# The left output projection of a segmented memory attention: from products of 256 columns to products of 512

## The chip, the cores and the metric

The kernel runs on one core of one Trainium2 chip. The metric is the device time of one execution in microseconds; the figure of a kernel is the median of its timed runs.

Five engines work from queues of their own: PE (matrix products, with the weight loads listed apart as PEld), DVE (the vector engine), ACT (the scalar engine), POOL (GpSimd) and SP, which here only issues transfers. PE adds its products up in PSUM; DVE and ACT read PSUM, POOL and the transfers do not, so what POOL works on has to lie in SBUF, the on-chip working memory.

## The reference, cut to what matters

A layer-normed sequence `xn` of 2048 rows and 1024 columns goes through two branches that are added to `x`. Branch A is attention over 64 segments of 32 rows, with 8 memory rows in front of each; the attention output of the memory rows is the memory of the next segment, so the segments depend on each other in a chain.

```python
for s in range(n_seg):                                  # 64 segments
    h = concat([mem, xs], axis=1)                       # 8 memory rows + 32 rows
    q, k, v = h @ Wq, h @ Wk, h @ Wv                    # 32 heads of 128
    p = softmax(where(mask, q @ k.T * scale, -1e9))
    o = einsum('bhte,hed->btd', p @ v, Wo)              # output projection
    mem = o[:, :M, :].copy()
    outs.append(o[:, M:, :])
...
return x + A(xn, mem0, ...) + B(xn, ...)
```

Branch B takes the two rows of `xn` with the highest routing score through a gated feed-forward of 3584 and adds the result to these two rows.

## The kernel before, in words

**Tiling.** A segment's step takes 32 rows, the 8 memory rows and the first 24 of its own 32 rows; the last 8 rows of a segment (its "left" rows) do not fit into a tile of 32 and are set apart. The left rows of four consecutive segments make one more tile of 32 rows; such a set of four is called a group (G), and j = 0 to 3 is the segment's place in it. The weights are cut into 64 granules of 128 partitions x 2048 columns: granules 0 to 47 are Wq, Wk and Wv in six phases of eight (`PHASES`), granules 48 to 63 are Wo, two heads each. 44 granules stay in SBUF for the whole run; the 20 of `STREAMED` come in anew for every segment, through five slots (the tile `g`). SP issues them in a fixed order, each as soon as a slot is free.

**A segment's step.** For each phase p and granule kc, four products of 32 rows x 512 columns go to four groups of 32 PSUM rows (line 788, `PSm`); they run at the same time on four strips of PE's columns. Then ACT casts `PSm` to bf16 (`XB`, line 807), PE transposes it in the next phase, and the scores of a head half are formed at (2, 6) and (4, 6), their exponent taken on ACT (line 666) and softened on DVE (lines 671 to 694) at (3, 4) and (5, 0). The pair (p, kc) names a place in the program: what is hooked there is issued behind the products of granule 8p + kc. After phase 5 come the 16 granules of Wo (place (6, w)), written to `WO` by `project`, line 574: eight products of 256 columns per granule. Line 856 adds `WO` to the input rows; this is the last DVE work of the step, and the next segment's memory comes out of it.

**The left rows.** Their projections are made from granules that are in SBUF anyway, as extra passes between the products of the main rows. The table `PASSES` says at which place (j, p, kc) which granules are passed; a unit ("q0", "k0" and so on, and "o" for the output projection) has one PSUM bank, `psL`, and the units follow each other in it. `COPIES` says where a finished unit is taken out of the bank. Unit "o" begins in the fourth segment of a group, in (6, 3) to (6, 14) with five passes, goes on with three at (7, 0) and two at (8, 0), that is, around the end of the segment, and is finished in the next group's first segment (j = 0) with six more. In the last segment of all, the sixteen passes of "o" stand between those of `WO`, and the sum follows at the end.

**The left output projection, before.** `one_pass` calls the same `project` as the main rows, with `lhs_left` (line 578) as weights: for each of a granule's two heads, four products of 256 columns, one for each quarter of the 1024 output columns, to rows 32 g to 32 g + 31 of the tile `WL`. Rows 32 g hold columns 256 g to 256 g + 255. `copy_unit` at (0, 4, 3) adds the bank to `OL`, which holds the left rows of x in the same arrangement (`load_left`, `sum_left`), in one DVE operation (line 596), and POOL stores four blocks (line 599).

**What sets the order.** The schedule is written by hand: every engine runs its instructions in the order in which the code issues them. Tiles of one name tag share one buffer (`one` is a pool with one buffer for each tag), so a tile may be written only when the last reader of the tile before it in that tag is done. `OTL`, the attention output of the left rows, is in tag "otl"; `OL` and `STL`, the next group's left rows as weights, share the tag "stl".

Of the kernel before, what the change touches and what calls it, by code (L numbers as in the profile page):

```python
# [8 lines left out]
BF16 = mybir.dt.bfloat16  # L9
F32 = mybir.dt.float32  # L10
U32 = mybir.dt.uint32
ALU = mybir.AluOpType
# [31 lines left out]
}  # L44

COPIES = {"q0": (1, 1, 0, "scalar"), "q1": (1, 5, 7, "vector"), "k0": (2, 2, 0, "scalar"), "k1": (3, 1, 0, "scalar"),
          "v0": (3, 4, 7, "scalar"), "v1": (3, 5, 7, "scalar"), "o": (0, 4, 3, "vector")}


@with_exitstack  # L50
def kernel(
# [16 lines left out]
    nc = tc.nc  # L68
    P = 128
    Bsz, S, D = A_x.shape  # L70
    H, E = A_Wq.shape[1], A_Wq.shape[2]
    M = A_mem0.shape[1]
    SEG = int(A_seg_len)
# [9 lines left out]
    XM = SEG - M  # L83
# [34 lines left out]
    one = ctx.enter_context(tc.tile_pool(name="one", bufs=1, reuse_waits="tile"))  # L118
# [78 lines left out]
    for s in range(4):  # L197
        nc.vector.tensor_copy(out=SELM[:, s, :, 0:XM],
                              in_=IDENT[:, 32 * s:32 * s + XM].unsqueeze(1).to_broadcast([P, 4, XM]))
        nc.vector.tensor_copy(out=SELL[:, s, :, :],  # L200
                              in_=IDENT.rearrange("p (s c) -> p s c", c=32)[:, :, XM:SEG])
# [113 lines left out]
        PTm = turn(OB)  # L315
        nc.vector.tensor_copy(out=gview(st)[:, :, :, XM:SEG], in_=PTm[:, :, :, XM:SEG])

    def load_left(G, t):
        o4 = x2[4 * G * SEG:4 * (G + 1) * SEG, :].rearrange("(s r) d -> s r d", s=4)
        for g in range(4):  # L320
            nc.gpsimd.dma_start(out=t[32 * g:32 * (g + 1), :], in_=o4[:, XM:SEG, 256 * g:256 * (g + 1)])
        return t

    def norm_left(t, G):
# [230 lines left out]
    def one_pass(u, g, Gv):  # L555
        if u not in units:
            begin(u)
        PS, n = units[u]
        units[u][1] = n - 1
        if u == "o":  # L560
            project(PS, g - 48, Gv, lhs_left, n == 1, first=(n == 16))
        else:
            left_pass(PS, g, Gv, n == 8, n == 1)

# [5 lines left out]
    def project(PS, w, Gv, lhs, last, first=False):  # L570
        for hs in range(2):
            h = 2 * w + hs
            for g in range(4):
                nc.tensor.matmul(PS[32 * g:32 * g + 32, 0:256], lhsT=lhs(h),  # L574
                                 rhs=Gv[:, D * hs + 256 * g:D * hs + 256 * (g + 1)], start=(first and hs == 0),
                                 stop=(last and hs == 1), tile_position=(0, 32 * g), skip_group_check=True)

    def lhs_left(h):
        return otl_of[0][:, h, :, :].rearrange("p s r -> p (s r)")

    xl_of, otl_of = [None], [None]

    def copy_unit(u, s, engine):
        PS, n = units.pop(u)
        assert n == 0, (u, s, n)
        Gu = group_of(u, s)
        copy = nc.scalar.copy if engine == "scalar" else nc.vector.tensor_copy
        half = int(u[-1]) if u != "o" else 0
        if u[0] == "v":
            new_vl[half] = one.tile([P, 512], BF16, tag=roles[half], name="VL")  # L590
            copy(out=new_vl[half][:, :], in_=PS[:, :])
            if half:
                roles.insert(0, roles.pop())
        elif u == "o":
            OL = xl_of[0]
            nc.vector.tensor_tensor(out=OL[:, :], in0=PS[:, 0:256], in1=OL[:, :], op=ALU.add)
            o4 = out2[4 * Gu * SEG:4 * (Gu + 1) * SEG, :].rearrange("(s r) d -> s r d", s=4)
            for g in range(4):
                nc.gpsimd.dma_start(out=o4[:, XM:SEG, 256 * g:256 * (g + 1)], in_=OL[32 * g:32 * (g + 1), :])
        else:  # L600
            XBl = one.tile([P, 512], BF16, tag=roles[0], name="XBl")
            copy(out=XBl[:, :], in_=PS[:, :])
            stores.append(lambda: nc.scalar.dma_start(out=ql_d[Gu][2 * half + "qk".index(u[0])], in_=XBl[:, :]))
            if engine == "scalar":
                stores.pop()()

    for s in range(NSEG):
# [227 lines left out]
        for w in range(16):  # L835
            if w == 5:
                attend(1, 0)
            if w == 8 and s + 1 < NSEG:
                attend(1, 1, lambda: turned.append(turn_rows(xn, left_too)))
                nxt["st"], stl = new_st(turned[0])  # L840
                STL = stl or STL
            elif w == 8:
                attend(1, 1)
            Gv = granule(48 + w)
            project(WO, w, Gv, lhs_main, w == 15, first=(w == 0))
            held[48 + w] = Gv
            run_passes(6, w)
            if w == 9 and s + 1 < NSEG:
                new_lx(s + 1)
                bring_back(1, nc.scalar.copy)  # L850
                bring_back(2, nc.vector.tensor_copy)
            if w == 11 and j == 3:
                xl_of[0] = load_left(G, one.tile([P, 256], BF16, tag="stl", name="OL")[:, :])
            release(6, w)
        OB = X[s % 2]
        nc.vector.tensor_tensor(out=OB[:, :], in0=WO[:, 0:256], in1=OB[:, :], op=ALU.add)  # L856
# [127 lines left out]
```

## Time and profile before

| | |
|---|---|
| median of 3 timed runs | 1893.73 us (1885.0 to 1897.26) |
| profiled execution, its own time | 1889.55 us |
| its span from first to last instruction | 1887.9 us |
| PE busy / weight loads busy | 1574.1 us (83%) / 882.6 us (47%) |
| DVE / ACT / POOL busy | 880.0 / 681.9 / 441.4 us |
| moved by DMA | 712.41 MB, mean 377 GB/s |
| streamed granules | 1134 transfers of 512 KB, 63 of 256 KB |
| granted PE clock, mean | 0.955 |

The page is one profiled execution. Busy shares are averages over stretches with different limits, so stretches of single segments are read too: a table of windows gives, for each, its length, the busy time and the number of instructions of each engine, the granted clock, the share of time that the 16 DMA engines were busy, and the rate. In lists, "[1.17 <-DMA g<-wsc]" behind an instruction means that its engine stood idle for 1.17 us before it and that the transfer into `g` ended that; "issue" stands where the profile names nothing that the engine waited for. Tile names are the program's (`WL<-g,OTL` writes WL from g and OTL), shapes are partitions x elements.

### The profile page before, as it was taken

The page shows a single profiled execution, that of the slowest core. Times are in us where ns is not written, and L with a number is a line of the kernel's source. Part 1 is how long each engine was busy: PE and PEld are TensorE (multiplying, and loading weights), DVE is VectorE, ACT ScalarE, POOL GpSimd, SP SyncE. Part 2 cuts the span into 40 slices and gives each one's busy share as a digit, 9 for nine tenths or more (in the row PEclk, how much of TensorE's full clock was granted, in tenths as well). Part 3 has the DMA queues.
Part 4 walks back from the last instruction along what each step waited for, and adds up shares of the span by engine and source line. Part 5 has one row for each costly group of instructions (what it writes and reads, how often), then busy time and mean ns, then how long its engine had stood idle before and what let it go on. Part 6 is the DMA issues. An engine that isn't in the chain of part 4 may idle for free.

```text
span 1887.9 us, 82457 instructions
## 1 busy us (share of the span) xinstructions
PE 1574.1 (83%) x36000; PEld 882.6 (47%) x36000; DVE 880.0 (47%) x2913; ACT 681.9 (36%) x1916; POOL 441.4 (23%) x882
## 2 busy tenths in 40 slices
PE   3458889888888898888888988888998888989864
PEld 1134545454454444545454544545454454545433
DVE  6725444545354444544454344445544454455430
ACT  1123433344334343433333334333433443434320
POOL 3111223222131322213121321312132131312220
PEclk8669999999999999999999999999999999999995
DMA  9999999999999999999999999999999999999998
GB/s 369 400 363 381 366 384 383 395 388 371 364 374 394 354 387 384 378 389 363 394 374 381 367 359 371 362 391 368 381 375 367 381 383 382 372 392 380 389 406 327
DMA packets 232122, 712.41 MB, mean 377 GB/s; under 512 B 39296, under 2 KB 53168, under 8 KB 231760
## 3 DMA queue, kind: packets, MB, share of 16 engines
q1 hardware_dynamic: 194384, 671.18, 93.0%
q0 software_dynamic: 28736, 28.09, 4.7%
q10 hardware_dynamic: 8640, 7.87, 1.2%
q8 instruction: 282, 4.62, 0.9%
q14 instruction: 80, 0.66, 0.1%
HBM read 694.32 MB, written 22.29 MB: 380 GB/s over the span
## 4 chain that ended last, share of the span: by engine, by line
DMA 57%; PE 38%; DVE 2%; issue 2%; SPq 0%; ACT 0%; ACTq 0%; DVEq 0%
DMA g<-wsc 50%; PE PSm L788 21%; PE PSl L567 5%; PE WO L574 5%; PE BT L624 3%; PE WL L574 2%; DMA XP<-in_A_x_dram 2%; DMA MW<-in_B_w_gate_dram 1%; DMA MW<-in_B_w_up_dram 1%; DVE XR L248 1%; DMA g<-in_A_Wq_dram 1%; DMA wres<-in_A_Wo_dram 1%; DMA g<-in_B_w_down_dram 1%; DMA g<-in_A_Wo_dram 1%; PE BT L293 1%
## 5 line engine op out<-in xcount | busy, mean ns | idle before, releaser
L788 PE MATMUL PSm<-wres,ST 128*32 128x512 bf16 x8448 | 706.7, 384 | 10.6 <-issue 4.0
L788 PEld LDWEIGHTS <-ST 128*32 128x32 bf16 x12288 | 326.0, 96 | 402.7 <-issue 172.9
L788 PE MATMUL PSm<-g,ST 128*32 128x512 bf16 x3588 | 362.6, 387 | 101.0 <-DMA g<-wsc 75.5
L574 PEld LDWEIGHTS <-OT 128*32 128x32 bf16 x8192 | 221.2, 98 | 159.6 <-issue 140.2
L807 ACT CAST XB<-PSm 128x512 bf16<-128x512 f32 x256 | 150.1, 586 | 309.7 <-PE PSm L788 306.8
L574 PE MATMUL WO<-wres,OT 128*32 128x256 bf16 x5632 | 240.7, 281 | 17.5 <-issue 8.8
L483 POOL DMA_DIRECT2D LX<-ql_d x63 | 33.6, 533 | 813.7 <-PE WO L574 339.2
L574 PE MATMUL WO<-g,OT 128*32 128x256 bf16 x2560 | 134.4, 284 | 83.8 <-DMA g<-wsc 73.7
L567 PE MATMUL PSl<-wres,STL 128*32 128x512 bf16 x2112 | 184.2, 389 | 0.0
L858 POOL DMA_DIRECT2D out_dram<-X x256 | 129.5, 513 | 217.9 <-DVE X L856 174.6
L639 DVE COPY KT<-BT 128x512 bf16<-128x512 bf16 x112 | 45.9, 410 | 282.5 <-ACT XB L807 114.5
L273 POOL DMA_DIRECT2D X<-in_A_x_dram x256 | 129.6, 510 | 183.8 <-PE PSm L788 70.7
L377 ACT COPY BK<-KEPT 128x512 bf16<-128x512 bf16 x126 | 74.3, 590 | 135.0 <-PE WO L574 98.5
L632 ACT COPY QT<-BT 128x512 bf16<-128x512 bf16 x128 | 74.9, 585 | 121.4 <-PE BT L490 69.0
L567 PEld LDWEIGHTS <-STL 128*32 128x32 bf16 x3072 | 84.4, 98 | 55.0 <-issue 9.4
L856 DVE TENSOR_TENSOR X<-WO,X 128x256 bf16<-128x256 f32 x64 | 27.2, 425 | 177.7 <-PE WO L574 177.7
L624 PEld LDWEIGHTS <-XB 128*128 128x128 bf16 x1024 | 58.6, 98 | 106.1 <-ACT XB L807 58.7
L817 ACT CAST VM<-PSm 128x512 bf16<-128x512 f32 x128 | 75.8, 592 | 83.1 <-PE PSm L788 81.4
L624 PE MATMUL BT<-IDENT,XB 128*128 128x128 bf16 x1024 | 102.4, 223 | 2.4 <-ACT QKL L502 1.4
L710 PEld LDWEIGHTS <-VM 32*128 32x128 bf16 x2048 | 65.1, 91 | 83.4 <-issue 68.4
L656 DVE TENSOR_TENSOR BS<-BS,CT 128x96 f32<-128x96 f32 (+1 forms) x256 | 59.6, 233 | 83.6 <-PE BS L649 79.2
L381 DVE COPY g<-KEPT 128x512 bf16<-128x512 bf16 x126 | 47.6, 420 | 108.8 <-PE PSm L788 61.6
(171 smaller groups left out, 2361.0 us busy)
## 6 DMA issues: line engine op xcount, KB each, us to landing
g<-wsc SPq DMA_DIRECT2D x1134, 512.0 KB, 6.0
g<-wsc SPq DMA_DIRECT2D x63, 256.0 KB, 5.4
LX<-ql_d POOLq DMA_DIRECT2D x63, 128.0 KB, 5.8
ql_d<-XBl ACTq DMA_DIRECT2D x60, 128.0 KB, 5.7
MW<-in_B_w_gate_dram SPq DMA_DIRECT2D x16, 448.0 KB, 9.2
MW<-in_B_w_up_dram SPq DMA_DIRECT2D x16, 448.0 KB, 9.2
wres<-in_A_Wk_dram SPq DMA_DIRECT2D x12, 512.0 KB, 11.3
MW<-in_B_w_down_dram SPq DMA_DIRECT2D x12, 512.0 KB, 10.4
```

What stands on the lines that cost most here:

```text
L273: nc.gpsimd.dma_start(out=X[s % 2][32 * g:32 * g + XM, :], in_=x2[s * SEG:s * SEG + XM, 256 * g:256 * (g + 1)])
L377: copy(out=back[c][:, :], in_=KEPT_COLS[KEPT_WHOLE][c])
L567: nc.tensor.matmul(PSl[32 * jq:32 * jq + 32, :], lhsT=STL[:, g % KC, :], rhs=part(Gv, jq), start=first_, stop=last_, tile_position=(0, 32 ...
L574: nc.tensor.matmul(PS[32 * g:32 * g + 32, 0:256], lhsT=lhs(h), rhs=Gv[:, D * hs + 256 * g:D * hs + 256 * (g + 1)], start=(first and hs == ...
L624: nc.tensor.transpose(out=PTq[:, il, :, :].rearrange("p j r -> p (j r)"), in_=XB[:, il * P:(il + 1) * P], identity=IDENT[:, :])
L632: nc.scalar.copy(out=QT[half][:, :, :], in_=pv)
L656: nc.vector.tensor_tensor(out=S4, in0=S4, in1=m, op=ALU.add)
L710: nc.tensor.matmul(o, lhsT=VM[half][q0:q0 + 32, il * P:(il + 1) * P], rhs=PTm[q0:q0 + 32, il, 0:NK], start=True, stop=False, tile_position ...
L788: nc.tensor.matmul(PSm[32 * jq:32 * jq + 32, :], lhsT=ST[:, kc, :], rhs=part(Gv, jq), start=(kc == 0), stop=(kc == KC - 1), tile_position= ...
L807: nc.scalar.copy(out=XB[:, :], in_=PSm[:, :])
L817: nc.scalar.copy(out=VM[half][:, :], in_=PSm[:, :])
L858: nc.gpsimd.dma_start(out=out2[s * SEG:s * SEG + XM, 256 * g:256 * (g + 1)], in_=OB[32 * g:32 * g + XM, :])
```

## The change

The left output projection gets a function of its own. Each head of a granule now has two products of 512 columns, which is the full width of the bank. Even heads go to rows 0 to 63 (columns 0 to 511 in rows 0 to 31, 512 to 1023 in rows 32 to 63), odd heads to rows 64 to 127 in the same way, so that the four products of a granule stand on the four strips of PE. Even and odd heads are thus summed in different rows, and the two halves have to be added once per group: ACT copies one half of each across to the other rows into a new f32 tile `LF` (in tag "otl"), DVE adds the half that lies in place, and POOL adds `LF` to `OL` and stores. The blocks of 256 columns now stand in the order 0, 2, 1, 3, so `OL` is loaded "crossed" and stored likewise. In `PASSES` the six last passes stand earlier, and the sum moves from (0, 4, 3) to (0, 3, 3).

```diff
-          (3, 8, 0): [52, 54], (0, 1, 5): [55], (0, 2, 2): [57], (0, 2, 5): [58], (0, 3, 2): [60], (0, 3, 5): [61],
-          (0, 4, 2): [63]},
+          (3, 8, 0): [52, 54], (0, 0, 7): [55], (0, 1, 3): [57], (0, 1, 7): [58], (0, 2, 3): [60], (0, 2, 6): [61],
+          (0, 3, 2): [63]},
...
-          "v0": (3, 4, 7, "scalar"), "v1": (3, 5, 7, "scalar"), "o": (0, 4, 3, "vector")}
+          "v0": (3, 4, 7, "scalar"), "v1": (3, 5, 7, "scalar"), "o": (0, 3, 3, "vector")}
...
-    def load_left(G, t):
+    def load_left(G, t, crossed=False):
         o4 = x2[4 * G * SEG:4 * (G + 1) * SEG, :].rearrange("(s r) d -> s r d", s=4)
         for g in range(4):
-            nc.gpsimd.dma_start(out=t[32 * g:32 * (g + 1), :], in_=o4[:, XM:SEG, 256 * g:256 * (g + 1)])
+            b = 2 * (g % 2) + g // 2 if crossed else g
+            nc.gpsimd.dma_start(out=t[32 * g:32 * (g + 1), :], in_=o4[:, XM:SEG, 256 * b:256 * (b + 1)])
...
-            project(PS, g - 48, Gv, lhs_left, n == 1, first=(n == 16))
+            project_left(PS, g - 48, Gv, n == 16, n == 1)
...
+    def project_left(PS, w, Gv, first, last):
+
+        for hs in range(2):
+            lhsT = otl_of[0][:, 2 * w + hs, :, :].rearrange("p s r -> p (s r)")
+            for c in range(2):
+                r0 = 64 * hs + 32 * c
+                nc.tensor.matmul(PS[r0:r0 + 32, :], lhsT=lhsT, rhs=Gv[:, D * hs + 512 * c:D * hs + 512 * (c + 1)],
+                                 start=first, stop=last, tile_position=(0, r0))
...
-            nc.vector.tensor_tensor(out=OL[:, :], in0=PS[:, 0:256], in1=OL[:, :], op=ALU.add)
+            LF = one.tile([P, 256], F32, tag="otl", name="LF")
+            for c in range(2):
+                nc.scalar.copy(out=LF[64 * c:64 * c + 64, :], in_=PS[64 - 64 * c:128 - 64 * c, 256 * c:256 * c + 256])
+            for c in range(2):
+                here = slice(64 * c, 64 * c + 64)
+                nc.vector.tensor_tensor(out=LF[here, :], in0=PS[here, 256 * c:256 * c + 256], in1=LF[here, :], op=ALU.add)
+            nc.gpsimd.tensor_tensor(out=OL[:, :], in0=LF[:, :], in1=OL[:, :], op=ALU.add)
             o4 = out2[4 * Gu * SEG:4 * (Gu + 1) * SEG, :].rearrange("(s r) d -> s r d", s=4)
             for g in range(4):
-                nc.gpsimd.dma_start(out=o4[:, XM:SEG, 256 * g:256 * (g + 1)], in_=OL[32 * g:32 * (g + 1), :])
+                b = 2 * (g % 2) + g // 2
+                nc.gpsimd.dma_start(out=o4[:, XM:SEG, 256 * b:256 * (b + 1)], in_=OL[32 * g:32 * (g + 1), :])
...
-                xl_of[0] = load_left(G, one.tile([P, 256], BF16, tag="stl", name="OL")[:, :])
+                xl_of[0] = load_left(G, one.tile([P, 256], BF16, tag="stl", name="OL")[:, :], True)
```

The change moves instructions on PE, ACT, DVE and POOL; the line numbers of the changed kernel are 1 to 14 higher. On PE, where a group's first segment (j = 0) has the pass of granule 55, the program of before has it behind phase 1's sixth granule, and the pass (here its first two products of eight) reads:

```order
L788 LDWEIGHTS ST
L788 MATMUL PSm<-g,ST 32x512
L574 LDWEIGHTS OTL
L574 MATMUL WL<-wres_1127,OTL 32x256
L574 LDWEIGHTS OTL
L574 MATMUL WL<-wres_1127,OTL 32x256
```

In the changed program it stands behind phase 0's last granule, and this is all of it, up to the first product of phase 1:

```order
L802 MATMUL PSm<-wres_228,ST 32x512
L587 LDWEIGHTS OTL
L587 MATMUL WL<-wres_1127,OTL 32x512
L587 LDWEIGHTS OTL
L587 MATMUL WL<-wres_1127,OTL 32x512
L587 LDWEIGHTS OTL
L587 MATMUL WL<-wres_1127,OTL 32x512
L587 LDWEIGHTS OTL
L587 MATMUL WL<-wres_1127,OTL 32x512
L802 LDWEIGHTS ST
L802 MATMUL PSm<-wres_232,ST 32x512
```

The pass has moved six granules ahead and has eight instructions where it had sixteen; PE's whole program has 69,954 rows instead of 72,002.

On ACT, in the same segment, the rows from phase 2's cast (`XB`) to the keys (`KT`) of the second head half are, before:

```order
L807 CAST XB<-PSm 128x512
L632 COPY QT<-BT 128x512
L666 ACTIVATE BS<-BS 128x320
L807 CAST XB<-PSm 128x512
L637 COPY KT<-QKL 128x16x8
```

And in the changed program:

```order
L821 CAST XB<-PSm 128x512
L646 COPY QT<-BT 128x512
L605 COPY LF<-WL 64x256 x2
L680 ACTIVATE BS<-BS 128x320
L821 CAST XB<-PSm 128x512
L651 COPY KT<-QKL 128x16x8
```

The two copies of the sum stand between the copy of the queries and the exponent of the first head half. DVE's two additions (line 608) stand likewise in front of the softening, behind which the one addition of before stood, and POOL's addition (line 609) directly in front of the four stores of `OL`.

More of the change, by code (lines that the diff above doesn't have):

```diff
@@ L576, in project @@
                                  stop=(last and hs == 1), tile_position=(0, 32 * g), skip_group_check=True)
-    def lhs_left(h):
-        return otl_of[0][:, h, :, :].rearrange("p s r -> p (s r)")
     xl_of, otl_of = [None], [None]
+    def project_left(PS, w, Gv, first, last):
[5 more added lines that the diff above has]
+                                 start=first, stop=last, tile_position=(0, r0))
     def copy_unit(u, s, engine):
```

## The prediction

> **What bounds the kernel now.** I read the page first, then the list of who waited for whom on PE, then a table of stretches cut at the additions of line 856 (one a segment), then PE's timeline where the stretches differ.
>
> ```profile
> span 1887.9 us, 82457 instructions
> PE 1574.1 (83%) x36000; PEld 882.6 (47%) x36000; DVE 880.0 (47%) x2913; ACT 681.9 (36%) x1916; POOL 441.4 (23%) x882
> DMA 57%; PE 38%; DVE 2%; issue 2%; SPq 0%; ACT 0%; ACTq 0%; DVEq 0%
> q8 instruction: 282, 4.62, 0.9%
> PE PSm L788 <- DMA g<-wsc: 75.5, 172, 2.6
> PE WO L574 <- DMA g<-wsc: 73.7, 154, 1.9
> PE WL L574 <- issue: 10.1, 6, 2.3
> PE WO L574 <- issue: 9.4, 10, 2.7
> PE PSm L788 <- issue: 7.2, 7, 2.2
> ```
>
> The third row says that the chain that ended last runs alternately through weight transfers and PE; the two rows "<- DMA g<-wsc" (total us, times, longest) are 149.2 us in which PE stood still for a streamed granule. The three "<- issue" rows are 26.7 us in which PE waited for nothing the profile names. What that is, the end of the kernel shows, where PE does nothing but tiny products of two columns:
>
> ```profile
> 1853.89 3.57 PE L929 MATMUL GU<-T,MW 128*128 128x2 bf16 x128 [1.85 <-issue]
> 1860.10 3.57 PE L929 MATMUL GU<-T,MW 128*128 128x2 bf16 x128 [2.64 <-issue]
> 1866.32 1.20 PE L929 MATMUL GU<-T,MW 128*128 128x2 bf16 x39 [2.64 <-issue]
> ```
>
> 128 matmuls with their 128 weight loads, 256 instructions, take 3.57 us, then PE stands 2.64 us, and the next 256 come 6.21 us after the last (1860.10 to 1866.32). Queue q8 carries 282 packets; PE has 36,000 matmuls and 36,000 weight loads, and 72,000 / 282 is again 256. So PE's program arrives in pieces of 256, and a piece that is used up in under some 6.2 us is followed by a stop until the next is there. The Trainium skill ("Runtime: NRT & Kernel Launch", Instruction fetch mechanics) has the pieces of 256 but calls their cost mostly hidden; this trace agrees with the size and not with the hiding.
>
> Where this falls in the body:
>
> ```profile
> 856.30:885.30 29.00, 23.20 (x566) 13.74 (x558) 13.43 (x48) 10.43 (x30) 10.59 (x20) 1.00 0.99 363
> 885.30:911.40 26.10, 23.57 (x544) 13.01 (x540) 12.74 (x42) 10.06 (x29) 4.92 (x10) 1.00 1.02 391
> 911.40:937.00 25.60, 22.48 (x524) 12.16 (x520) 12.13 (x41) 10.33 (x29) 4.70 (x10) 1.00 1.02 390
> 937.00:964.70 27.70, 25.60 (x607) 14.37 (x603) 12.41 (x44) 11.19 (x31) 7.05 (x14) 1.00 1.00 384
> 964.70:991.40 26.70, 22.93 (x569) 13.78 (x561) 13.45 (x49) 10.53 (x31) 9.65 (x18) 1.00 1.01 368
> 1723.70:1749.90 26.20, 22.80 (x560) 13.20 (x551) 12.89 (x45) 10.33 (x29) 7.44 (x15) 1.00 1.01 385
> ```
>
> Columns: length, then busy time and count of PE, PEld, DVE, ACT, POOL, then granted clock, DMA share, GB/s. The first four rows are one group (the segments j = 0, 1, 2, 3), the last two are j = 0 of other groups. j = 1 and 2 have 1084 and 1044 PE instructions, j = 3 and 0 have 1210 and 1124: they hold the left output projection. Where j = 0 has no issue stop above 0.2 us (the last two rows) it lasts 26.2 to 26.7 us; the first row, 29.0 us, has two:
>
> ```profile
> 853.85 0.39 PE L574 MATMUL WL<-g,OTL 128*32 128x256 bf16 x8
> 854.73 0.39 PE L574 MATMUL WL<-g,OTL 128*32 128x256 bf16 x8
> 856.04 0.83 PE L574 MATMUL WL<-wres,OTL 128*32 128x256 bf16 x24
> 858.92 0.27 PE L293 MATMUL BT<-IDENT,X 128*128 128x128 bf16 x2 [2.05 <-issue]
> 859.12 0.62 PE L574 MATMUL WL<-wres,OTL 128*32 128x256 bf16 x16
> 872.14 0.40 PE L788 MATMUL PSm<-wres,ST 128*32 128x512 bf16 x3 [1.20 <-issue]
> ```
>
> 2.05 and 1.20 us stopped, and 2.3 to 2.8 us longer: a stop is passed on at about three quarters to one. The DMA rate falls in that row (363 against 390 GB/s), so the transfers do not run ahead meanwhile.
>
> **The change part by part.** *Products of 512 columns.* The price on PE is a pass of one granule:
>
> ```profile
> 325.61 0.39 PE L788 MATMUL PSm<-g,ST 128*32 128x512 bf16 x4
> 325.83 0.39 PE L574 MATMUL WL<-wres,OTL 128*32 128x256 bf16 x8
> 326.04 0.82 PE L788 MATMUL PSm<-wres,ST 128*32 128x512 bf16 x12
> ```
>
> Four products of 512 columns hold PE for 0.22 us (325.61 to 325.83), eight of 256 for 0.21 (325.83 to 326.04). The new pass has the form of the first, so 16 passes in each of 16 groups save nothing: 256 x 0.00. What falls is the count: 16 instructions a pass become 8, 128 fewer a group, 2048 in all, 8 pieces of 256. At 6.21 us a piece, half a piece less a group is at most 3.1 us a group or 50 us, more than there are stops, so the upper bound is the 26.7 us. The lower bound is zero, if the stops merely move. Between them: the piece that ended before 858.92 holds eight of these passes or so (five between the WO passes, three in the 24 matmuls of 856.04). Freed of 64 instructions, it takes in 64 others before the next stop is due: eight 512-column passes (8 instructions, 0.22 us) are 1.7 us more of work, four WO passes (16 instructions in the same time) 0.9 us. Not every group's pieces are cut so that they hold eight; I take the lower price, 0.85 us, for 15 groups: -13 us.
>
> *Passes moved.* Six passes of j = 0 go from phases 1 to 4 into phases 0 to 3; all are resident granules, so no slot is released sooner or later, and PE's work is only reordered: 0.
>
> *The sum at (3, 3) of j = 0.* Before, one DVE addition stood at (4, 3), behind the first softening. Now two ACT copies and two DVE additions stand at (3, 3) in front of exponent and softening, and one POOL addition in front of the four stores. The rows of that place (ACT, DVE and PE, in one group):
>
> ```profile
> 331.01 0.59 ACT L632 COPY QT<-BT 128x512 bf16<-128x512 bf16 x1 [0.87 <-PE BT L624]
> 331.49 0.43 ACT L666 ACTIVATE BS<-BS 128x320 f32<-128x320 f32 x1
> 332.17 0.59 ACT L807 CAST XB<-PSm 128x512 bf16<-128x512 f32 x1 [0.25 <-PE PSm L788]
> 331.95 0.49 DVE L671 TENSOR_REDUCE DN<-BS 128x8 f32<-128x320 f32 x1 [0.63 <-ACT BS L666]
> 334.03 0.39 DVE L596 TENSOR_TENSOR OL<-WL,OL 128x256 bf16<-128x256 f32 x1
> 334.46 0.21 PE L647 MATMUL BS<-KT,QT 128*32 128x40 bf16 x4 [0.16 <-ACT KT L639]
> 336.69 0.40 PE L788 MATMUL PSm<-g,ST 128*32 128x512 bf16 x4 [1.17 <-DMA g<-wsc]
> ```
>
> No copy of 64x256 from PSUM is in the trace. The nearest rows bound it:
>
> ```profile
> L719 ACT CAST OT<-WO 128x128 bf16<-128x128 f32 x128 | 34.1, 266 | 59.3 <-PE BT L712 58.6
> L807 ACT CAST XB<-PSm 128x512 bf16<-128x512 f32 x256 | 150.1, 586 | 309.7 <-PE PSm L788 306.8
> L734 POOL MEMSET BX<- 128x256 bf16 x15 | 4.8, 319 | 10.3 <-PE PSm L788 10.2
> ```
>
> 0.27 to 0.59 us; at 256 elements I take 0.37 (between, nearer the first), so ACT is held 0.74 us, of which its 0.25 us of idle time before XB covers a part: XB comes some 0.5 us later, and with it the transposes and keys of phase 4, on which PE already waits 0.16 us at 334.46. Each DVE addition is 0.39 us by its own row (as many columns, half the rows; 0.2 at the least); they run while the exponent does, in the 0.63 us in which DVE stood idle, so softening starts about 0.9 us later, and its last reading of the scores falls at about 334.2, still ahead of 334.46. So PE loses about 0.5 us a group there, and 2.2 us later it waits 1.17 us for a granule anyway. That wait hides it; where a group has no such wait, 0.5 x 15 = 7.5 us. I take +2, bounds 0 and +7.5. Nothing is gained on this edit: the removed DVE addition waited for nobody.
>
> POOL's addition has only the memset as a neighbour, 0.32 us for as many elements written; with two inputs read I bound it by 0.3 and 2 us and take 0.8. Queued behind it on POOL are the four stores of OL and then the load of LX. The chain starts 2.5 us sooner than the old addition (331.5 against 334.03) and needs 0.74 + 0.78 + 0.8 = 2.3, so the stores leave when they did: 0. It would cost only beyond that. The Trainium skill ("GPSIMD Engine Reference", Engine selection) speaks against this edit: elementwise work with two inputs belongs on VectorE, GpSimd being about half as fast, and its 2.6 cycles an element at 1.2 GHz make an estimate of 0.55 us and a dispatch. By that price the sum is the same.
>
> *The end.* In the last segment the same chain of five operations replaces one and puts the selected rows' load 1.9 us later. The final products wait for their weights anyway:
>
> ```profile
> L942 PE MATMUL YP<-MW,T 128*2 128x256 bf16 x96 | 6.0, 382 | 6.3 <-DMA MW<-in_B_w_down_dram 5.4 <-DVE YP L936 0.9
> ```
>
> 5.4 us of waits cover 1.9: 0.
>
> Sum, against the profiled execution (1889.55 us, span 1887.9): 1889.6 - 13 + 2 = 1878.6, say **1879 us**. The three timed runs have a median of 1893.73, 4 us above the profiled one, so on their scale the forecast is 0.6 to 0.8% less. For this kernel I call 1%, 19 us, what a measurement can tell from no change; the three runs spread over 12 us.
>
> **The rivals.** *A, the forecast*: the stops shrink by half, 1871 to 1887 us (12 groups at 0.85 us and +7.5, or 15 at 1.2 us and 0). 45%.
>
> *B, nothing to be had.* A granule that PE reaches sooner is waited for: the 149.2 us of DMA waits take up the 13. For it: the DMA share of 0.99 to 1.02 in every stretch. Against it: stretches of j = 0 without stops are shorter, as shown. Time 1889.6 + 0 to 7.5: 1886 to 1897. The page of the skill on instruction fetch leads to the same time by another way, there being nothing to hide. 22%.
>
> *C, all stops go.* Then 26.7 us fall, and some stretches at a lower clock with them:
>
> ```profile
> 1070.90:1103.00 32.10, 26.61 (x564) 15.27 (x557) 13.43 (x49) 10.60 (x30) 10.24 (x19) 0.85 0.99 344
> ```
>
> This j = 0 has a granted clock of 0.85 and lasts 32.1 us, 5.4 to 5.9 more than the undisturbed ones, a part of it its own stop. Two such fewer, at 4.5 us beyond the stops: 1889.6 - 26.7 - 9 = 1854; range 1850 to 1868. Against it: the WO passes, 16 instructions in 0.22 us, stay as they are. 17%.
>
> *D, the wait of the new chain.* At (3, 3) ACT is held by both copies at their long end (1.18 us) and DVE by both additions behind them; XB, keys, second scores, exponent and softening all come late, and attention at (5, 4) with them. That is 1.18 - 0.25 on ACT, and 0.35 more where the second scores wait for the first softening: about 1.3 us a group on PE. It decides if the granule wait behind it (1.17 us) is not there, since the transfers meanwhile got ahead, and the stops only move: 1889.6 + 15 x 1.3 = 1909; range 1900 to 1915. 16%.
>
> **How the numbers follow.** The likeliest is A, 1879. The range 1856 to 1901 takes in A, B and most of C and leaves out D and C's end, about 2 in 10. Faster by over 1%: C and the low end of A, 0.17 + 0.17 = 0.34. Slower by over 1%: most of D, 0.14. Within 1%: 0.52.
>
> **What would show it.** PE's "<- issue" rows outside the final products fall from 26.7 to 12 to 15 us (B: as before, or the DMA rows grow by as much; C: under 5). j = 0 has 88 and j = 3 40 PE instructions fewer, and j = 0 with the first half of its stretch at more than 363 GB/s. A new-shape pass holds PE 0.21 to 0.22 us; 0.25 or more would cost 256 x 0.03 = 8 us. ACT's copies show 0.37 us, POOL's addition under 2 us, and PE's wait for KT before the second scores of j = 0 stays under 0.7 us; if it is over 1.2 us, D holds. The forecast is wrong if the stops stay as long although the instructions are fewer.

## The result, and the profile after

The changed kernel takes 0.9951 of the time of before (95% interval 0.9927 to 0.9975; medians 1884.74 against 1894.49 us, 22 runs each): 9 to 10 us faster, under the 1% that the prediction set as its bound. The profiled execution took 1878.39 us against 1889.55; a second one of the changed kernel, from a later measurement, took 1892.38 and is used below to see what one profile can tell. One execution of that measurement, at a granted clock of 0.647, took 2172.86 us and is left out of its ratio.

The page of the changed kernel (span; busy time, share and count by engine; the chain that ended last; the queue that brings the program) and its list of who waited for whom on PE (total us, times, longest):

```profile
span 1876.7 us, 80489 instructions
PE 1572.0 (84%) x34976; PEld 850.8 (45%) x34976; DVE 885.9 (47%) x2929; ACT 692.0 (37%) x1948; POOL 452.5 (24%) x898
DMA 57%; PE 37%; DVE 3%; issue 1%; ACT 1%; SPq 1%; ACTq 0%; DVEq 0%
q8 instruction: 274, 4.49, 0.9%
...
PE PSm L802 <- DMA g<-wsc: 77.8, 170, 2.3
PE WO L575 <- DMA g<-wsc: 70.2, 145, 1.7
PE BT L638 <- ACT XB L821: 7.8, 14, 0.6
PE GU L943 <- issue: 7.3, 3, 2.6
PE WO L575 <- issue: 7.2, 8, 2.3
PE PSm L802 <- issue: 2.4, 2, 1.4
PE WL L587 <- issue: 1.4, 2, 1.1
```

PE has 1024 matmuls and 1024 weight loads fewer and the queue q8 eight packets of 256 fewer, but PE's busy time is the same (1572.0 against 1574.1): as many columns are streamed. The three "<- issue" rows of the body, which the prediction added up to 26.7 us, are now 7.2 + 2.4 + 1.4 = 11.0. With the view's small rows the stops outside the final products (GU) fall from 30.3 to 14.8 us; this sum is called "stops" below. In the second execution of the changed kernel the same sums are 15.8 us for the three rows and 20.1 for all, so what the change takes out is 10 to 15 us. The waits for streamed granules are 148.0 us (155.0 in the second execution), 149.2 before: they took up nothing of what was freed in the one, up to 6 us in the other. New is the wait for XB, 7.8 us.

That these stops are waits for PE's program, the traces show in two ways beyond the sums. Counted in the order in which PE's matmuls and weight loads start (with the 180 rows of its sequencer), all 31 stops of the profile before and all 21 of the one after (those in the final products included) stand at the same place of the count of 256, at remainders 193 to 195. No stop stands elsewhere. And at each of them a packet on queue q8 (all have 16,384 bytes, 64 for each of 256 instructions) has ended 1.2 to 1.7 us before PE goes on.

The table of stretches, cut at the additions of line 870 (length, busy time and count of PE, PEld, DVE, ACT, POOL, clock, DMA share, GB/s), shows a whole group and j = 0 of another:

```profile
534.40:559.90 25.50, 22.29 (x523) 12.24 (x516) 13.84 (x49) 11.24 (x32) 10.35 (x19) 1.00 1.02 384
559.90:585.10 25.20, 23.44 (x544) 12.69 (x540) 12.66 (x42) 10.15 (x29) 4.89 (x10) 1.00 1.03 401
585.10:612.00 26.90, 22.93 (x524) 12.43 (x520) 12.13 (x41) 10.44 (x29) 4.72 (x10) 1.00 1.01 394
612.00:640.50 28.50, 25.39 (x584) 13.84 (x580) 12.46 (x44) 11.19 (x31) 7.04 (x14) 1.00 0.99 371
1066.30:1092.20 25.90, 23.15 (x523) 12.20 (x519) 13.77 (x49) 11.16 (x32) 10.34 (x19) 1.00 1.03 386
```

j = 0 has 1039 to 1042 PE instructions where it had 1124, and in these two stretches no stop of more than 0.22 us: 25.5 and 25.9 us at 384 to 386 GB/s, where the stretch shown of before, with 3.25 us of stops, took 29.0 at 363 and two without large stops 26.2 and 26.7. j = 3 still has 1164 where it had 1210, and there most of the stops that are left stand. This is the largest of them, on PE's timeline at the end of the fourth stretch:

```profile
640.04 0.38 PE L575 MATMUL WO<-wres,OT 128*32 128x256 bf16 x5 [2.27 <-issue]
640.16 0.90 PE L587 MATMUL WL<-wres,OTL 128*32 128x512 bf16 x12
```

It lies in the WO passes, sixteen instructions each, which the change left as they were. Added up by segment over the whole trace, the stops of j = 0 fall from 18.3 to 4.2 us (3.4 in the second execution), those of j = 3 from 10.9 to 8.4, but not in the second execution, where they are 12.6. The gain is in j = 0, and its length shows it: on average over 15 groups 27.97 us before, 27.22 and 27.07 after, which is 11 to 14 us in all for 14 to 15 us of stops.

The place of the sum in one group, from the timelines of ACT, DVE, POOL and PE:

```profile
544.93 0.59 ACT L646 COPY QT<-BT 128x512 bf16<-128x512 bf16 x1 [0.87 <-PE BT L638]
545.53 0.74 ACT L605 COPY LF<-WL 64x256 f32<-64x256 f32 x2
546.18 0.42 ACT L680 ACTIVATE BS<-BS 128x320 f32<-128x320 f32 x1
546.62 0.59 ACT L821 CAST XB<-PSm 128x512 bf16<-128x512 f32 x1
546.31 0.86 DVE L608 TENSOR_TENSOR LF<-WL,LF 64x256 f32<-64x256 f32 x2 [1.06 <-PE PSm L802]
547.20 0.49 DVE L685 TENSOR_REDUCE DN<-BS 128x8 f32<-128x320 f32 x1
547.25 0.66 POOL L609 TENSOR_TENSOR OL<-LF,OL 128x256 bf16<-128x256 f32 x1 [4.29 <-DVE LF L608]
547.26 0.40 PE L638 MATMUL BT<-IDENT,XB 128*128 128x128 bf16 x4 [0.57 <-ACT XB L821]
548.59 0.21 PE L661 MATMUL BS<-KT,QT 128*32 128x40 bf16 x4 [0.17 <-ACT KT L653]
```

The two copies hold ACT for 0.74 us, exponent and cast come that much later, and PE stands 0.57 us for XB; the second scores behind it wait no longer than before (0.17 us against 0.16). DVE's additions take 0.86 us together. The profile puts the 1.06 us before them down to PE, but they start as ACT's copies end (545.53 + 0.74). POOL's addition takes 0.66 us.

### The profile page after: what moved, and what is told of

Read it like the earlier page. It is cut to its first block, busy times and chain, and to the rows that moved or that the text cites. A ratio compares the mean times of both kernels' runs of the same rounds, so it can differ in the third digit from the quotient of the medians.

```text
span 1876.7 us, 80489 instructions
## 1 busy us (share of the span) xinstructions
PE 1572.0 (84%) x34976; PEld 850.8 (45%) x34976; DVE 885.9 (47%) x2929; ACT 692.0 (37%) x1948; POOL 452.5 (24%) x898
## 4 chain that ended last, share of the span: by engine, by line
DMA 57%; PE 37%; DVE 3%; issue 1%; ACT 1%; SPq 1%; ACTq 0%; DVEq 0%
DMA g<-wsc 50%; PE PSm L802 20%; PE PSl L568 5%; PE WO L575 4%; PE BT L638 3%; DMA XP<-in_A_x_dram 2%; PE WL L587 2%; DMA MW<-in_B_w_gate_dram 1%; DVE XR L248 1%; DMA MW<-in_B_w_up_dram 1%; DMA g<-in_A_Wq_dram 1%; DMA wres<-in_A_Wo_dram 1%; DMA g<-in_A_Wo_dram 1%; DMA MW<-in_B_w_down_dram 1%; DMA g<-in_B_w_down_dram 1%
```

## The experiments

Ratios are to the kernel before, with 95% intervals; from 6 to 12 executions of each experiment and 23 to 35 of the kernel before beside them. Stops and granule waits come from one profiled execution each. The changed kernel's own stops were 14.8 us in one execution and 20.1 in another, its granule waits 148.0 and 155.0, so differences under 5 us of stops or 7 us of granule waits are not read. The mean granted clock of a kernel's executions lies between 0.954 and 0.959, and among executions of one kernel 0.001 more goes with about 1 us less, so a difference of 0.002 between two ratios is not read as an effect.

| kernel | ratio | stops, us | granule waits, us |
|---|---|---|---|
| before | 1 | 30.3 | 149.2 |
| changed | 0.9951 (0.9927 to 0.9975) | 14.8 | 148.0 |
| changed, second measurement | 0.9946 (0.9917 to 0.9975) | 20.1 | 155.0 |
| products split into 256 | 1.0043 (1.0019 to 1.0067) | 34.2 | 136.8 |
| places alone | 1.0036 (1.0012 to 1.0061) | 40.0 | 148.6 |
| old places | 0.9978 (0.9951 to 1.0005) | 13.1 | 143.4 |
| sum later | 0.9963 (0.9936 to 0.9990) | 16.4 | 156.3 |
| no crossing sum | 0.9945 (0.9919 to 0.9971) | 16.9 | 161.7 |
| last addition on VectorE | 0.9979 (0.9958 to 1.0000) | 16.2 | 136.6 |
| halves in j = 2 | 0.9964 (0.9941 to 0.9987) | 27.9 | 145.6 |
| halves in j = 3 | 0.9988 (0.9962 to 1.0013) | 29.5 | 131.3 |
| passes spread | 0.9910 (0.9879 to 0.9941) | 16.3 | 149.7 |
| passes spread, again | 0.9929 (0.9903 to 0.9955) | 17.6 | 152.0 |

The theory: PE's program arrives in pieces of 256 instructions; the change makes it shorter where it is densest, so PE stops less often for the next piece. The rivals: the gain comes from the earlier places, from the products' shape as such, or is partly eaten by the new chain of sums.

**The products split into 256.** Everything as changed, but each product of 512 columns made as two of 256 into the same rows.

```diff
-        for hs in range(2):
-            lhsT = otl_of[0][:, 2 * w + hs, :, :].rearrange("p s r -> p (s r)")
-            for c in range(2):
-                r0 = 64 * hs + 32 * c
-                nc.tensor.matmul(PS[r0:r0 + 32, :], lhsT=lhsT, rhs=Gv[:, D * hs + 512 * c:D * hs + 512 * (c + 1)],
-                                 start=first, stop=last, tile_position=(0, r0))
+        for q in range(2):
+            for hs in range(2):
+                lhsT = otl_of[0][:, 2 * w + hs, :, :].rearrange("p s r -> p (s r)")
+                for c in range(2):
+                    r0, at = 64 * hs + 32 * c, D * hs + 512 * c + 256 * q
+                    nc.tensor.matmul(PS[r0:r0 + 32, 256 * q:256 * (q + 1)], lhsT=lhsT, rhs=Gv[:, at:at + 256],
+                                     start=(first and q == 0), stop=(last and q == 1), tile_position=(0, r0),
+                                     skip_group_check=True)
```

> Each of the changed kernel's products of 512 columns is made as two of 256 into the same rows, so that PE has the 72,000 instructions of the kernel before, while the places and the sum at (0, 3, 3) stay as changed. Theory (the gain is PE's shorter program): the issue stops outside the final products are back at 25 to 30 us (14.8 in the changed kernel), the new chain's wait stays, and the time is 1.000 to 1.008 of before. Rival (the gain comes from the earlier places, or from the shape of 512 columns as such on PE): with the places as the source the ratio stays at 0.995.

Measured: 1.0043, clear of 1 and of the changed kernel. Its issue rows on PE:

```profile
PE WO L575 <- issue: 13.3, 12, 2.7
PE WL L588 <- issue: 12.9, 8, 2.2
PE PSm L804 <- issue: 3.5, 6, 1.4
```

With the number of instructions back, the stops are back (34.2 us with the small rows, above the 25 to 30 that were expected), and the gain is gone. Places, sum and streamed columns are those of the changed kernel; what differs is the cut of the products, and with it the count. The price of a pass is not the source: where no wait interrupts it, a pass holds PE for 0.218 us here (median), 0.216 in the changed kernel and 0.218 before. Between the two kernels lie 0.92%, 17 us, for 14 to 19 us of stops. That this kernel is slower than the one before agrees with the next run, which has the same places and the same count.

**The places alone, and the old places.** The kernel before with the changed tables `PASSES` and `COPIES`, and the changed kernel with the tables of before.

```diff
-          (3, 8, 0): [52, 54], (0, 1, 5): [55], (0, 2, 2): [57], (0, 2, 5): [58], (0, 3, 2): [60], (0, 3, 5): [61],
-          (0, 4, 2): [63]},
+          (3, 8, 0): [52, 54], (0, 0, 7): [55], (0, 1, 3): [57], (0, 1, 7): [58], (0, 2, 3): [60], (0, 2, 6): [61],
+          (0, 3, 2): [63]},
...
-          ... "o": (0, 4, 3, "vector")}
+          ... "o": (0, 3, 3, "vector")}
```

> The kernel before, products of 256 and one DVE addition, with the changed places alone (sum at (0, 3, 3)). Theory: no gain, since PE's program has its old length: 0.997 to 1.003, issue stops 25 to 30 us. Rival (places): 0.995 or less.

Measured: 1.0036, slower, with 40.0 us of stops. The expectation of no difference missed: the stops rise by 9.7 us, beyond the 30 that had been expected. A likely reason is that passes of sixteen instructions, set nearer to the dense end of the segment before, make it denser; it is not shown, since of the 9.7 us only 2.4 fall into j = 0, where the passes moved, and 5.2 into j = 3. As the source of the gain the places are out.

The reverse, the changed kernel with the two rows marked "-":

> The changed kernel with the places of before: passes at (0, 1, 5) to (0, 4, 2), the sum at (0, 4, 3). Theory: PE has the same 69,952 instructions, the issue stops stay at 12 to 18 us; the copies now stand behind the keys' transposes, so PE's wait for ACT's XB (7.8 us in 14 times) goes, another one may come at the second scores: 0.990 to 0.996. Rival (the earlier places bring the gain): 1.000 or more.

Measured: 0.9978, with 13.1 us of stops as expected, but above the expected range; its interval reaches 1.0005, so this run alone shows no gain. The waits on PE that differ are these:

```profile
PE PSm L802 <- DMA g<-wsc: 91.5, 185, 2.5
PE WO L575 <- DMA g<-wsc: 51.9, 117, 1.7
PE WO L724 <- ACT OTL L735: 14.6, 15, 1.5
```

At (0, 4, 3) the chain of sums puts off the second softening and with it the attention at (5, 4): PE waits about 1 us a group for the copy into OTL, in all 14.6 us where the changed kernel has 1.3 and 3.5. In one group ACT stands 2.20 us for DVE before the exponent of the second head half (1.23 us in a group of the changed kernel), and the copies into OTL stand behind that exponent on ACT. No wait for XB is left. So the stops went and another wait came, almost as long. It comes with the sum's place and not with the passes': the last run below has the passes close to their old places, but the sum at (0, 4, 0), and waits for OTL 0 and 0.8 us. In time the difference from the changed kernel lies within the intervals.

**The sum later.** The changed kernel with the sum at (0, 4, 0), behind exponent and cast.

```diff
-          ... "o": (0, 3, 3, "vector")}
+          ... "o": (0, 4, 0, "vector")}
```

> The changed kernel with the sum hooked at (0, 4, 0) and not at (0, 3, 3): on ACT the two copies stand behind the exponent and behind the cast XB of phase 3, where ACT stood idle for 0.86 us before. Theory: PE's wait for XB at the transposes of phase 4 (7.8 us in 14 times) goes, the issue stops stay at 12 to 18 us, and the time falls by 3 to 8 us against the changed kernel: 0.990 to 0.994 of before. Rival (that wait is hidden by the wait for a granule behind it): 0.995 as the changed kernel, and PE's DMA waits grow by as much.

Measured: 0.9963, above the expected 0.990 to 0.994 and the changed kernel's time within the intervals; no row "<- ACT XB" is left in the view, but

```profile
PE PSm L802 <- DMA g<-wsc: 83.4, 177, 2.1
PE WO L575 <- DMA g<-wsc: 72.9, 152, 1.8
```

are together 8.3 us more than in the changed kernel's first execution, and the wait for XB was 7.8. The rival expected just that, but the second execution of the changed kernel, with its wait for XB, has 155.0 us as well: that PE now waits for granules instead is not shown by the waits. The time bears the rival out so far that, by the intervals, at most some 4.5 of the 7.8 us can have been gained.

**No crossing sum.** The two halves are not brought together: one VectorE addition takes the first 256 columns of the bank in all rows, and the other 256 columns, even heads' and odd heads' alike, are left out. PE's products are those of the changed kernel.

```diff
-            LF = one.tile([P, 256], F32, tag="otl", name="LF")
-            ...
-            nc.gpsimd.tensor_tensor(out=OL[:, :], in0=LF[:, :], in1=OL[:, :], op=ALU.add)
+            nc.vector.tensor_tensor(out=OL[:, :], in0=PS[:, 0:256], in1=OL[:, :], op=ALU.add)
```

> The changed kernel without its chain of sums: the odd heads of the left rows are left out, one VectorE addition takes the bank's first 256 columns, as before, at (0, 3, 3). It prices the chain of two copies, two additions and POOL's addition. Theory from the two runs on the sum's place (the wait for XB is hidden by the wait for a granule): 0.992 to 0.996, at most 4 us less than the changed kernel. Rival (the chain takes back what the shorter program gives, 0.5 us and more a group): 0.987 to 0.991.

Measured: 0.9945 against 0.9951 with the chain. The five operations cost about 1 us of the whole kernel, nothing that these runs can tell from zero, and at most some 8 us by the intervals.

**The last addition on VectorE.**

```diff
-            nc.gpsimd.tensor_tensor(out=OL[:, :], in0=LF[:, :], in1=OL[:, :], op=ALU.add)
+            nc.vector.tensor_tensor(out=OL[:, :], in0=LF[:, :], in1=OL[:, :], op=ALU.add)
```

> The changed kernel with the last addition (LF + OL) on VectorE and not on GpSimd. GpSimd takes 0.67 us for it, its engine idle before. Theory: GpSimd's longer time is covered, and VectorE's 0.3 to 0.4 us more stands in front of the softening: 0.994 to 0.998, the second scores' wait for KT or the first softening a little longer. Rival (GpSimd slows VectorE or its transfers): 0.992 or less.

Measured: 0.9979, inside the expected range, and not faster than with GpSimd; its interval overlaps the changed kernel's. The addition itself is shorter on VectorE, 0.43 us against 0.66. In its trace PE waits 7.2 us for OTL, in the changed kernel's two 1.3 and 3.5. The slower engine, idle for 4.29 us before its addition in the group shown, is no worse a place here; that it is the better one is not shown.

**Instructions put back elsewhere.** The changed kernel, with the main products of phases 0 and 1 cut into halves of 256 columns in one segment of each group: 128 instructions more a group, as many as the change took out. First in j = 2, then in j = 3.

```diff
+                cut = 2 if s > 0 and j == 2 and p < 2 else 1
+                n = 512 // cut
+                for q in range(cut):
-                for jq in range(4):
-                    nc.tensor.matmul(PSm[32 * jq:32 * jq + 32, :], lhsT=ST[:, kc, :], rhs=part(Gv, jq),
-                                     start=(kc == 0), stop=(kc == KC - 1), tile_position=(0, 32 * jq))
+                    for jq in range(4):
+                        nc.tensor.matmul(PSm[32 * jq:32 * jq + 32, n * q:n * (q + 1)], lhsT=ST[:, kc, :],
+                                         rhs=part(Gv, jq)[:, n * q:n * (q + 1)], start=(kc == 0 and q == 0),
+                                         stop=(kc == KC - 1 and q == cut - 1), tile_position=(0, 32 * jq),
+                                         skip_group_check=(cut == 2))
```

> The changed kernel with the 2048 PE instructions put back elsewhere: in each group's third segment (j = 2) the main products of phases 0 and 1 are made as two of 256 columns, 128 instructions more a group, as many as the change took out, in a stretch without issue stops. Theory (a stop comes only where 256 instructions are used up sooner than the next 256 arrive, some 5 to 6.2 us): the issue stops outside the final products rise from 14.8 us to 15 to 22, and the time is 0.994 to 0.999 of before. Rival (the length of PE's program costs as such, wherever it stands): as when the products were split in place, 34 us of stops and 1.002 or more.

Measured: 0.9964, in the expected range, but the stops rose to 27.9 us, more than the 15 to 22 expected:

```profile
PE WO L575 <- issue: 10.5, 15, 1.4
PE PSm L805 <- issue: 6.8, 10, 1.3
PE PSl L568 <- issue: 4.0, 5, 1.5
```

By segment, j = 2 has 8.2 us where the changed kernel has 0.2 and 1.9 in its two profiles: sixteen halved granules are 256 instructions in 3.5 us of work, a dense stretch of their own. The rival's 1.002 did not come: 8 to 13 us more of stops than in the changed kernel's profiles, and a time that these runs do not tell from it, though by the intervals it may be up to 9 us longer. So it is a question, and not a finding, whether a stop costs its length everywhere; j = 2 has the most granule waits (57 us in the changed kernel), j = 3 the fewest (14 to 16). Hence the next run:

> As the run with halves in j = 2, with the 128 instructions a group put into phases 0 and 1 of the fourth segment (j = 3). There PE waits for granules for 15 us in all, in j = 2 for 58 us. Theory (a stop costs time where PE is late anyway and is taken up where PE waits for granules behind it): stops of j = 3 rise from 8.7 us to 15 to 20, as those of j = 2 did from 0.1 to 8.2, but the time goes to 0.998 to 1.002 of before. Rival (a stop costs the same in every segment): 0.996 as with j = 2.

Measured: 0.9988, as the theory expected; stops 29.5 us, in j = 3 20.9, just above the 15 to 20 that were expected. That is 0.0024 above j = 2, but the intervals overlap (0.9962 to 1.0013 and 0.9941 to 0.9987): the direction is the expected one, the difference is not shown. The length of j = 3 shows that the stops cost time there: 27.97 us on average over 16 groups, against 26.95 and 27.27 in the changed kernel's two profiles, 11 to 16 us in all for 8 to 13 us of stops. For j = 2 the same comparison decides nothing: 27.04 against 26.64 and 26.89, in an execution in which the segments j = 1, where nothing was changed, were longer too (27.09 against 26.29 and 26.86). The granule waits of j = 2 fell there from 57 to 51 us.

**The passes spread.** The six passes of j = 0 two to six granules later than changed, the sum at (0, 4, 0).

```diff
-          (3, 8, 0): [52, 54], (0, 0, 7): [55], (0, 1, 3): [57], (0, 1, 7): [58], (0, 2, 3): [60], (0, 2, 6): [61],
-          (0, 3, 2): [63]},
+          (3, 8, 0): [52, 54], (0, 1, 1): [55], (0, 1, 5): [57], (0, 2, 2): [58], (0, 2, 5): [60], (0, 3, 1): [61],
+          (0, 3, 5): [63]},
...
-          ... "o": (0, 3, 3, "vector")}
+          ... "o": (0, 4, 0, "vector")}
```

> The changed kernel with the six passes of j = 0 two to six granules later, (0, 1, 1) to (0, 3, 5), close to where they stood before, and the sum at (0, 4, 0), behind the exponent and the cast. Theory: the stops around the segment's end get fewer (13.1 us with the old places against 14.8) and neither XB nor OTL is waited for: 0.991 to 0.996. Rival (the places are worth nothing to the end): 0.996, as with the sum at (0, 4, 0) alone.

Measured: 0.9910, the fastest of all. XB and OTL are not waited for, as expected; the stops, 16.3 us, are not fewer than the changed kernel's, so they do not explain its time. It was run again beside the changed kernel on the same chip:

> The changed kernel itself, beside the next one on the same chip: 0.993 to 0.998 of before, stops of 12 to 18 us.

> The kernel with the passes spread to (0, 1, 1) to (0, 3, 5) and the sum at (0, 4, 0), once more, to tell whether it beats the changed kernel. If the places matter: 0.988 to 0.994 and below the changed kernel of this call by 0.002 or more. If the first run was chance: 0.994 to 0.998, as the changed kernel.

Measured: 0.9946 for the changed kernel, its stops 20.1 us and not 12 to 18, and 0.9929 for the spread one. Both measurements of the spread kernel lie below both of the changed kernel, by 0.002 and 0.004, but the 0.002 that had been asked for side by side was missed (0.0017), and the intervals overlap. It is the best version of this study and faster than the one before by 0.7 to 0.9%; that it beats the changed kernel is likely and not shown.

## Why the prediction was right

*The price of a pass.* Right. On PE's timeline of the changed kernel the pass of four products of 512 columns holds PE for 0.21 us (540.20 to 540.41), as the eight of 256 did:

```profile
540.20 0.39 PE L587 MATMUL WL<-wres,OTL 128*32 128x512 bf16 x4
540.41 0.39 PE L802 MATMUL PSm<-wres,ST 128*32 128x512 bf16 x4
```

*The stops.* Right in kind, and in size within what two profiles of one kernel differ by: 13 us were forecast to go; 15.7 went in the three rows that the forecast summed and 15.5 in all rows by the first profile, 10.9 and 10.2 by the second. They went where the forecast looked for them, in j = 0. The split products show the cause by putting the count back. Two steps of the working do not hold. The piece that ended before 858.92 holds six of the passes and not eight: the stop of 0.20 us that ends the piece before it comes after the first two of them.

```profile
853.13 0.17 PE L710 MATMUL BT<-PT,VM 32*128 32x40 bf16 x1 [0.20 <-issue]
```

With six, the same reckoning gives three WO passes, 0.66 us a group and 10 us in all. And "a piece that is used up in under some 6.2 us is followed by a stop" is not so in the trace it was read from: of the 156 pieces that PE used up in under 6.2 us between the first and the last addition of line 856, 27 were followed by a stop, of the 35 under 5 us 18. 6.21 us is the spacing in the final products alone. Case C, that all stops go, did not come, for the reason given against it: the WO passes keep theirs.

*The way to the end.* The sum took each us of stop for a us of time, although its own example had given 2.3 to 2.8 us for 3.25, which is 0.7 to 0.86. The split kernel gives 17 us for 14 to 19, the change as a whole 9 us for 10 to 15.5, j = 0 alone 11 to 14 us for 14 to 15, the halves in j = 3 11 to 16 us for 8 to 13. So most of a stop's length reaches the end; whether less of it does where PE waits for granules, as in j = 2, stays open. B, that granule waits take everything up, is refuted by the time: it needed 1886 us or more, a ratio of 0.998, and the interval ends at 0.9975.

*The new chain.* PE's wait for XB was forecast at 0.5 us a group and hidden by the granule wait behind it; it is 0.57 us, in 14 groups 7.8 us. Two runs without it are not faster, by the intervals by less than 4.5 us (sum later) and 8 us (no crossing sum), so a good part of it is hidden. The +2 us of the sum was about 1, not told from zero. ACT's copies were put at 0.37 us each and take 0.37 (0.74 for two), DVE's additions at 0.39 each and take 0.42. POOL's addition was put at 0.8 us and takes 0.66. The estimate from the Trainium skill ("GPSIMD Engine Reference", Performance versus the Vector engine) was 0.55 us and a dispatch; the trace, with 0.66 us, agrees. D did not come: the second scores wait 0.17 us. Its mechanism exists, though: with the sum at (0, 4, 3) PE waits 14.6 us for OTL.

*The moved passes.* "PE's work is only reordered: 0" was the weakest step. In the old form the same move, with the sum at (0, 3, 3), costs 0.36% (interval 0.12 to 0.61) and 9.7 us of stops. The prediction looked at the slots that a move releases and not at what it does to the stops. At equal places, by contrast, the shorter program, its new chain included, gains 0.85% (0.9951 against 1.0036), some 16 us, where the forecast has 11. Taken in the other order, the shorter program with the sum at its old place gains 0.22%, not clear of zero, and the new places 0.27% more. So the terms of the sum do not simply add, and that the total came out within 2 us of the forecast is in part luck.

*The end.* Put at 0. The waits for the final weights are there, now 7.0 us, but from the last addition of line 870 to the last instruction the two profiles of the changed kernel take 59.4 and 59.2 us, the one before 58.0. The split kernel, with the same chain, takes 57.7, so the chain is not the reason; what is stays open.

The forecast ratio, 1879 to 1889.55, is 0.9944; 0.9951 was measured. In the chances, "faster by over 1%" was given 0.17 for the low end of A, which A's own range, 1871 to 1887, hardly reaches: 1% is reached at 1870.6.

## What to carry to other kernels

Count an engine's instructions per stretch, beside their time. Here PE's program came in pieces of 256, and a piece that PE used up in under 5 us was followed by a stop in 18 of 35 cases before the change; wider products, which bring fewer instructions for as many columns, shortened the kernel although PE streams as much. A stop of this kind is told from other waits by two signs: nothing that the profile names ended it, and all of them stand at the same place of the count of 256. Moving work into a dense place can cost time even if it is only reordered: 0.36% here. A wait that the profile shows on the bounding engine may be worth little to remove while a transfer is waited for right behind it: the run without that wait of 7.8 us won nothing that shows, and at most some 4.5. And a sum from one profile of each kernel is good to a few us only: two profiles of the same kernel had 14.8 and 20.1 us of stops.

## What the runs showed of the hardware that had not been expected

Stops arise where the program is made dense: halving sixteen granules in a segment that had 0.2 and 1.9 us of stops in two profiles gave it 8.2. In all thirteen profiles of this study every stop on PE that the profile calls "issue" stands at remainder 193 to 195 of the count of 256, and PE goes on 1.1 to 1.7 us after a packet of 16,384 bytes on q8 has ended. That packet starts, for nine in ten pieces of the profile before, only 1.1 to 4.1 us after PE has entered the piece before, and takes 0.9 to 1.6 us; so the program is ahead of PE by about one piece, and a fast piece ends in a stop where the packet of the next one started too late for it. What sets that start was not tried. Where PE stopped for over 0.4 us in that profile, 4.6 to 7.4 us passed from one piece to the next. Only in the final products, which use up piece after piece in 3.57 us, is the spacing steady, 6.21 to 6.22 us, as before:

```profile
1840.24 3.57 PE L943 MATMUL GU<-T,MW 128*128 128x2 bf16 x128 [2.04 <-issue]
1846.46 3.57 PE L943 MATMUL GU<-T,MW 128*128 128x2 bf16 x128 [2.64 <-issue]
1852.67 1.20 PE L943 MATMUL GU<-T,MW 128*128 128x2 bf16 x39 [2.64 <-issue]
```

The 16 DMA engines are busy all through that stretch (DMA share 1.02 to 1.04). Whether that spacing is shorter with idle transfers was not tried.
